# A fused attention and gated-MLP kernel: four engines in a hand-written order instead of one

## The chip, the cores and the metric

The kernel runs on one core of one Trainium2 chip. The metric is the device time of one execution in microseconds (us); lower is better. The profile gives a "span" (first to last instruction), which is about 2 us shorter than the time. The engines are named as in the profile: PE (TensorE, matrix multiplication), PEld (its weight loads), DVE (VectorE), ACT (ScalarE), POOL (GpSimd) and SP (SyncE, here used only to issue DMAs).

## The reference, cut to what matters

```python
# q, k, v: (B=8, H=8, S=576, D=64);  w_in: (512, 2048);  w_out: (2048, 512)
theta = pi/2 * arange(S) / S
phi(x) = concat([relu(x)*cos(theta), relu(x)*sin(theta)], axis=-1)   # 64 -> 128 features
kv  = einsum('bhsf,bhsd->bhfd', phi(k), v)          # per batch and head, 128 x 64
z   = sum over s of phi(k)
num = einsum('bhsf,bhfd->bhsd', phi(q), kv)
den = einsum('bhsf,bhf->bhs',  phi(q), z) + 1e-6
x   = (num / den), heads put side by side           # (4608 tokens, 512)
h   = x @ w_in
out = (h * cos(h)) @ w_out
```

Batches are independent of each other in the attention, so batch b+1's attention can be computed while batch b goes through the MLP. A batch has 576 tokens: four tiles of 128, and 64 left over, which two batches share as one "remainder" tile.

## The kernel before: the parts that the change touches

The work is organised in stages. Stage s runs the first layer (x @ w_in and the gate) of batch s, the second layer of batch s-1, and, placed between their matmuls, the attention of batch s+1. A first-layer tile is four matmuls of 512 columns, a second-layer tile is sixteen. The features and casts that the attention needs are these:

```python
def prep(b, name, dst, t):                 # features of k or q, one token tile
    in_ = raw[name][:, :, t, :]
    for g in range(2):                     # g=0: cos, g=1: sin
        sc = CS[:, b % 2, g, t:t + 1]
        if b == 0 and g == 1 and t % 5 in (0, 1, 3, 4):
            nc.scalar.activation(out=dst[:, t, :, g, :], in_=in_, func=AF.Relu, scale=sc)
        else:
            nc.vector.tensor_scalar(out=dst[:, t, :, g, :], in0=in_, ..., op0=ALU.max, op1=ALU.mult)

def prep_v(b):                             # v to f16; only batch 0 uses ScalarE
    for t in range(NT + 1):
        ...
        if b == 0 and t % 2 == 1: nc.scalar.activation(out=dst, in_=src, func=AF.Copy)
        else:                     nc.vector.tensor_copy(out=dst, in_=src)

def kv_group(b, hb):                       # needs the k features and v of all five token tiles
    ...
    for hh in range(HB):
        for t in range(NT + 1):
            nc.tensor.matmul(KV[:, hh, :], lhsT=kp[:, t, h]..., rhs=V1[b % 2][:, t, h, :], ...)

def gate(dst, M1, n):                      # h * cos(h), the cosine as a shifted sine
    nc.scalar.activation(out=ch[:, 0:n], in_=M1, func=AF.Sin, bias=PIH, scale=1.0)
    nc.vector.tensor_tensor(out=dst, in0=M1, in1=ch[:, 0:n], op=ALU.mult)
```

Only TensorE's order is written by hand; a scheduler orders the other engines. The attention's steps are spread over the MLP's steps by their number:

```python
for name in ("k", "q", "v"): ...           # first loads
...
with tc.manual_schedule(engines={mybir.EngineType.PE}):
    ...                                     # opening: batch 0's attention, first layer, batch 1's attention
    for s in range(1, B + 1):
        side = attention(s + 1) if s + 1 < B else []
        spread(mlp(s), (xr if s == 1 else []) + list(side))
```

## Time and profile before

| | before |
|---|---|
| time, median of 3 runs first taken | 328.23 us (327.62 to 328.58) |
| span of the profiled run | 325.8 us, mean granted TensorE clock 0.988 |
| busy | PE 291.2, DVE 204.8, ACT 145.2, POOL 7.9 us |
| stage 1 starts / stage 2 starts / last matmul ends | 69.95 / 97.73 / 321.0 us |

These are lines of the first parts of the profile's page for the kernel before: the span, the busy times, and three rows in which each digit is a fortieth of the span (8.1 us). The PE and ACT rows give the busy share in tenths, the PEclk row the clock that TensorE was granted, in tenths of full speed.

```profile
span 325.8 us, 5431 instructions
PE 291.2 (89%) x2100; PEld 153.1 (47%) x2100; DVE 204.8 (63%) x520; ACT 145.2 (45%) x225; POOL 7.9 (2%) x19
...
PE   0578799989679979999999999999989999999994
...
ACT  2844273566253524454454442554444444554111
...
PEclk9999899999799999999999999999999999999999
```

The PE row is 9 almost everywhere after the twelfth slice (one 7, at 114 to 122 us): from 98 us on, TensorE is the bound, and what can be gained there is small. The losses lie in front. The timeline of the kernel before shows them. Its columns are the start in us, the duration in us, the engine, the line of the kernel, the operation with its tiles and count, and in brackets how long the engine had idled before and what released it.

```profile
11.88 1.04 PE L135 MATMUL QP_0_124<-IDENT,qp_106 128*128 128x128 f16 x8 [11.88 <-ACT qp_106 L96]
...
37.25 0.88 DVE L98 TENSOR_SCALAR kp_334<-km,CS 128x512 f16<-128x512 f32 x2 [11.31 <-DMA km<-in_k_dram]
38.78 1.87 PE L237 MATMUL M_403<-xT_108,w_in_sb 128*128 128x512 f16 x4 [2.42 <-DVE g_338 L230]
...
85.71 0.30 PE L160 MATMUL NUM_0_0_978<-kvz_795,qT_849 128*128 128x65 f16 x4 [2.54 <-DMA qT_849<-qp_794]
97.73 1.02 PE L237 MATMUL M_1176<-xT_796,w_in_sb 128*128 128x512 f16 x4 [2.17 <-DMA xT_796<-x_3_1072]
```

DVE sat 11.31 us in batch 1's first k feature, whose data had not arrived, with batch 0's gates queued behind it; TensorE ran out of free output buffers (the program has eight) and waited 2.42 us. The tile after that wait took 1.87 us; a first-layer tile at full clock is listed with 1.02 to 1.04 us, or 0.865 us from start to start. In stage 1 TensorE waited 2.54 us for q transposed and, at the start of stage 2, 2.17 us for x transposed, both by DMA.

### The profile page before, as it was taken

The page shows a single profiled execution, that of the slowest core. Times are in us where ns is not written, and L with a number is a line of the kernel's source. Part 1 is how long each engine was busy: PE and PEld are TensorE (multiplying, and loading weights), DVE is VectorE, ACT ScalarE, POOL GpSimd, SP SyncE. Part 2 cuts the span into 40 slices and gives each one's busy share as a digit, 9 for nine tenths or more (in the row PEclk, how much of TensorE's full clock was granted, in tenths as well). Part 3 has the DMA queues.
Part 4 walks back from the last instruction along what each step waited for, and adds up shares of the span by engine and source line. Part 5 has one row for each costly group of instructions (what it writes and reads, how often), then busy time and mean ns, then how long its engine had stood idle before and what let it go on. Part 6 is the DMA issues. An engine that isn't in the chain of part 4 may idle for free.

```text
span 325.8 us, 5431 instructions
## 1 busy us (share of the span) xinstructions
PE 291.2 (89%) x2100; PEld 153.1 (47%) x2100; DVE 204.8 (63%) x520; ACT 145.2 (45%) x225; POOL 7.9 (2%) x19
## 2 busy tenths in 40 slices
PE   0578799989679979999999999999989999999994
PEld 0553245554354534445554544445734544446441
DVE  2941499599699699494977595578943752444000
ACT  2844273566253524454454442554444444554111
POOL 0800000000000000000000000000000000000000
PEclk9999899999799999999999999999999999999999
DMA  7999954929957968993599667963920241010221
GB/s 231 292 206 205 288 171 148 328 93 255 291 118 175 260 218 205 227 274 110 131 195 268 206 177 163 262 206 90 186 82 32 35 113 64 2 64 2 80 80 64
DMA packets 78680, 53.73 MB, mean 165 GB/s; under 512 B 47424, under 2 KB 76096, under 8 KB 78656
## 3 DMA queue, kind: packets, MB, share of 16 engines
q1 hardware_dynamic: 74144, 49.16, 54.6%
q0 software_dynamic: 4224, 4.19, 7.8%
q8 instruction: 16, 0.26, 0.3%
q10 hardware_dynamic: 288, 0.04, 0.1%
q14 instruction: 8, 0.07, 0.1%
HBM read 36.74 MB, written 9.44 MB: 142 GB/s over the span
## 4 chain that ended last, share of the span: by engine, by line
PE 66%; DVE 11%; DMA 9%; issue 6%; ACT 2%; POOL 1%; DVEq 0%; POOLq 0%
DMA qT_849<-qp_794 3%; DVE g_338 L230 3%; DMA qT_1216<-qp_1168 3%; DMA km<-in_k_dram 1%; ACT ch L229 1%; DVE kp_334 L98 1%; DVE qp_1581 L98 1%; PE M_723 L271 1%; PE M_2316 L271 1%; PE M_1458 L271 1%; DVE g_1175 L230 1%; PE M_3657 L271 1%; PE M_3618 L271 1%; PE M_3251 L271 1%; PE M_3168 L271 1%
## 5 line engine op out<-in xcount | busy, mean ns | idle before, releaser
L237 PEld LDWEIGHTS <-w_in_sb 128*128 128x128 f16 x512 | 49.1, 100 | 65.4 <-issue 14.0
L249 PEld LDWEIGHTS <-w_in_sb 128*128 128x128 f16 x256 | 14.6, 98 | 0.9
L98 DVE TENSOR_SCALAR kp_334<-km,CS 128x512 f16<-128x512 f32 x10 | 4.7, 476 | 11.3 <-DMA km<-in_k_dram 11.3
L135 PE MATMUL QP_0_124<-IDENT,qp_106 128*128 128x128 f16 x8 | 1.0, 311 | 11.9 <-ACT qp_106 L96 11.9
L271 PEld LDWEIGHTS <-g_806 128*128 128x128 f16 x64 | 6.3, 98 | 8.0 <-issue 0.7
L271 PEld LDWEIGHTS <-g_338 128*128 128x128 f16 x64 | 5.9, 98 | 8.4 <-DVE g_338 L230 1.3
L271 PEld LDWEIGHTS <-g_3290 128*128 128x128 f16 x64 | 6.3, 98 | 7.6
L135 PEld LDWEIGHTS <-qp_106 128*128 128x128 f16 x40 | 4.1, 147 | 12.2 <-ACT qp_106 L96 11.9
L271 PEld LDWEIGHTS <-g_1588 128*128 128x128 f16 x64 | 6.3, 98 | 7.5 <-issue 0.2
L271 PEld LDWEIGHTS <-g_1175 128*128 128x128 f16 x64 | 6.2, 98 | 7.3
L271 PEld LDWEIGHTS <-g_2033 128*128 128x128 f16 x64 | 6.2, 98 | 7.3
L271 PEld LDWEIGHTS <-g_2891 128*128 128x128 f16 x64 | 6.2, 98 | 7.3
L271 PEld LDWEIGHTS <-g_2446 128*128 128x128 f16 x64 | 6.2, 98 | 7.3
L108 DVE CAST V_1_72<-vm 128x512 f16<-128x512 f32 x20 | 7.2, 420 | 0.0
L98 DVE TENSOR_SCALAR kp_793<-km,CS 128x512 f16<-128x512 f32 x10 | 4.4, 480 | 3.9 <-PE KV_1_619 L116 3.9
L108 DVE CAST V_0_71<-vm 128x512 f16<-128x512 f32 x18 | 6.4, 420 | 0.0
L98 DVE TENSOR_SCALAR qp_1581<-qm,CS 128x512 f16<-128x512 f32 x10 | 4.2, 477 | 3.1 <-DMA qT_1216<-qp_1168 3.1
L98 DVE TENSOR_SCALAR kp_105<-km,CS 128x512 f16<-128x512 f32 x6 | 2.5, 482 | 5.4 <-DMA km<-in_k_dram 5.4
L98 DVE TENSOR_SCALAR qp_2884<-qm,CS 128x512 f16<-128x512 f32 x10 | 4.2, 476 | 1.9 <-DMA qT_2495<-qp_2439 1.9
L98 DVE TENSOR_SCALAR qp_1168<-qm,CS 128x512 f16<-128x512 f32 x10 | 4.4, 474 | 1.2 <-DMA qT_849<-qp_794 1.2
L230 DVE TENSOR_TENSOR g_3290<-M_3291,ch 128x512 f16<-128x512 f32 x1 | 0.7, 692 | 7.1 <-ACT ch L229 7.1
L98 DVE TENSOR_SCALAR qp_2439<-qm,CS 128x512 f16<-128x512 f32 x10 | 4.1, 479 | 1.5 <-DMA qT_2074<-qp_2026 1.5
(893 smaller groups left out, 721.1 us busy)
## 6 DMA issues: line engine op xcount, KB each, us to landing
out_dram<-ost SPq DMA_DIRECT2D x32, 256.0 KB, 2.4
km<-in_k_dram SPq DMA_DIRECT2D x8, 640.0 KB, 5.1
qm<-in_q_dram SPq DMA_DIRECT2D x8, 640.0 KB, 4.9
vm<-in_v_dram SPq DMA_DIRECT2D x8, 640.0 KB, 7.2
km<-in_k_dram SPq DMA_DIRECT2D x8, 512.0 KB, 5.4
qm<-in_q_dram SPq DMA_DIRECT2D x8, 512.0 KB, 5.4
vm<-in_v_dram SPq DMA_DIRECT2D x8, 512.0 KB, 8.6
w_in_sb<-in_moe_w_in_dram POOLq DMA_DIRECT2D x4, 512.0 KB, 8.8
```

The costliest lines, as they stand in the source:

```text
L98: nc.vector.tensor_scalar(out=dst[:, t, :, g, :], in0=in_, scalar1=0.0, scalar2=sc, op0=ALU.max, op1=ALU.mult)
L108: nc.vector.tensor_copy(out=dst, in_=src)
L135: nc.tensor.matmul(QP[:, h, :], lhsT=src[:, h].rearrange("p g d -> p (g d)"), rhs=IDENT, is_transpose=True)
L229: nc.scalar.activation(out=ch[:, 0:n], in_=M1, func=AF.Sin, bias=PIH, scale=1.0)
L230: nc.vector.tensor_tensor(out=dst, in0=M1, in1=ch[:, 0:n], op=ALU.mult)
L237: nc.tensor.matmul(M1, lhsT=w_in_sb[:, c, j * P:(j + 1) * P], rhs=xts[b][:, c, :], start=(c == 0), stop=(c == NCT - 1))
L249: nc.tensor.matmul(M1[:, jj, :], lhsT=w_in_sb[:, c, j * P:(j + 1) * P], rhs=xts[("r", pr)][:, c, :], start=(c == 0), stop=(c == NCT - 1))
L271: nc.tensor.matmul(M2, lhsT=gts[key][:, j, gsl], rhs=w_out_sb[:, j, :], start=(j == 0), stop=(j == NJT - 1))
```

## The change

The intent: close those holes. All four engines get a written order; the loads go k, v, q; batch 0's first layer begins on the first two token tiles; one second-layer tile (two in stage 1) is kept for each stage's end, to cover the transposes there; the attention's steps are placed by the TensorE time that has passed. To take load off DVE, half of the k features and all casts of v go to ScalarE in every stage. Stores move to GpSimd's queue, and the last tile's eviction is split between two engines. The core of the diff:

```diff
+    late = []                       # gate multiplies and num/den divisions are put off by one step
+    def flush(): ...
-    def prep(b, name, dst, t): ...
-    def prep_v(b): ...
+    def feat(b, name, t, g, act): ...          # act: on ScalarE, else on VectorE
+    def val(b, t, act): ...
...
-        nc.vector.tensor_tensor(out=dst, in0=M1, in1=ch[:, 0:n], op=ALU.mult)
+        flush()
+        late.append(lambda: nc.vector.tensor_tensor(out=dst, in0=M1, in1=ch[:, 0:n], op=ALU.mult))
...
-    def moe1(b, j):
+    def moe1(b, j, s0=0, s1=SM):               # first layer on a part of the tokens
...
+            eng = nc.sync if b == B - 1 else nc.gpsimd
...
     def spread(main, side):
-        (by number of steps)
+        side, at = list(side), 0.0
+        for us, f in main:
+            while side and side[0][0] <= at:
+                side.pop(0)[1]()
+            f()
+            at += us
...
-    for name in ("k", "q", "v"):
+    for name in ("k", "v", "q"):
...
-    with tc.manual_schedule(engines={mybir.EngineType.PE}):
+    with tc.manual_schedule(engines={ET.PE, ET.DVE, ET.Activation, ET.SP}):
+        ...                                     # opening, written out
+        for s in range(1, B + 1):
+            M1_US, M2_US, b = 0.87, 3.46, s + 1
+            m1 = [(M1_US, lambda j=j: moe1(s, j)) for j in range(NJT)] if s < B else []
+            ahead = 2 if s == 1 else 1
+            m2 = [(M2_US, lambda t=t: moe2_main(s - 1, t)) for t in range(2 if s == 2 else 1, NT)] if s > 1 else []
+            ...                                 # one m2 step after every `per` m1 steps
+            if s < B:
+                main += [(M2_US, lambda t=t: moe2_main(s, t)) for t in range(ahead)]
+            ...
+                for t in T1:
+                    side += [(1.1 * t, lambda t=t: feat(b, "q", t, 0, False)),
+                             (1.1 * t, lambda t=t: feat(b, "q", t, 1, False)),
+                             (6.5 + t, lambda t=t: feat(b, "k", t, 0, False)),
+                             (6.5 + t, lambda t=t: feat(b, "k", t, 1, True)),
+                             (7.0 + t, lambda t=t: val(b, t, True))]
+                side += [(5.5, lambda: q_trans_dma(b)), (5.6, lambda: load(b + 1, "q")),
+                         (11.6, lambda: load(b + 1, "k")), (11.6, lambda: load(b + 1, "v")),
+                         (13.0, lambda: kv_group(b, 0)), (14.0, lambda: kv_group(b, 1))]
+                side += [(16.5 + 1.3 * t, lambda t=t: num(b, t)) for t in range(NT + b % 2)]
+            side.sort(key=lambda x: x[0])
+            spread(main, side)
```

## The prediction

> **What bounds the kernel now.** The page gives a span of 325.8 us (median time 328.23), PE busy 291.2 (89%), DVE 204.8, ACT 145.2; the chain of waits is 66% PE. The PE timeline shows where PE is not busy: nothing before 11.88 us (first q transpose); cold matmuls until 31 us (a first-layer tile takes 1.6-1.9 us instead of 0.865); 2.42 us at 36 us, because DVE sat 11.3 us in a feature op waiting for batch 1's k while batch 0's gates queued behind it, and 1.7 us of slow clock after; in stage 1 (69.95-97.73) 2.54 us for qT, 2.17 us for xT, about 1.4 us of slow clock; 4.9 us after the last matmul. From 97.7 to 321.0 PE has only 5-6 us of holes.
>
> **What the change does.** TensorE work is nearly equal. Opening: k, v, q order lets KV start near 11.6 us; the first layer starts near 24 us on two token tiles (27.07 before); gates no longer sit behind batch 1's features, so batch 0's first layer should end near 40.5 us (47.2 before). Then ACT has five 1.0 us qT copies and two V casts ahead of KV, so about 2 us go again: stage 1 starts near 63.5 (69.95 before). Gain 6.5 us. Tail: split eviction and smaller stores, about 1 us. Waits for qT and xT are covered by a second-layer tile moved to each stage's end (worth 5-6 us), except at the end of stage 1, where x of three tiles is made inside one 3.46 us tile: 2-2.5 us stay.
>
> **What it costs.** Half of the k features and all V casts move from DVE to ACT, in a fixed order. On ACT one feature starts 0.62 us after the last, a V cast 0.52, a sine 0.60 (ACT timeline). In stages 2, 3 and 5 all ten stand behind the eviction of a second-layer tile. From that tile's end ACT needs 0.2+0.53+5x0.62+5x0.52+2 or 3 sines, 7.6-8.2 us, before the last V is cast; PE has only 4 or 5 first-layer tiles (3.5-4.3 us) before KV, which needs all five. Estimate: PE waits 4 us in stages 2, 3, 5, 2.5 us in 4 and 6, 3.5 us in stage 1: 17 us in stages 2-6 that the old order did not have. [...] here 2.42 us of idle was followed by tiles of 1.87 and 1.72 us. I add 0-7 us, 3 in the middle.
>
> **Sum (span).** 63.5 + stage 1 34.3 (now with two second-layer tiles) + stages 2-8 210 of work + 17 of waits + 3.7 tail = 328.5, plus 3 clock = 331; time = span + 2.4. Without the waits on ACT it would be about 313. Weighing that, I say 330 us, 8 in 10 between 316 and 341. Faster by over 2% 0.25, within 2% 0.43, slower 0.32.
>
> **What would show it.** PE timeline: in each of stages 1-6 an idle of 2.5-4 us at the first KV group, released by the ACT cast of V; tiles over 1.2 us right after. DVE busy down about 25 us, ACT up by the like. First layer starts at 22-25 us; no 11 us DVE wait for km; no PE wait on qT after stage 1; stores on the software DMA queue without effect.
>
> **What would make it wrong.** PE late at KV for other reasons, which hides the wait, or ACT casts cheaper: then 313-320. Clock dropping after every wait[...]: 340.

63.5 + 34.3 + 210 + 17 + 3.7 is 328.5 us, and with 3 us for the clock it was put at 331 us of span, or 333.4 us of time.

## The result, and the profile after

The changed kernel took 341.44 us (median of 4 runs, 339.96 to 343.24) against 328.40 us (327.62 to 328.65) for the kernel before on the same chip: the ratio is 1.040, with a 95% interval of 1.035 to 1.046, so it is slower. All eight runs are fast. Ratios in this document are the mean time of one kernel's fast runs over that of the other's in the same rounds, so they are not quite the ratio of the medians quoted. The predicted 330 us was too low, and 341.44 lies just outside the range of 316 to 341.

The same lines of the page, for the kernel after:

```profile
span 338.1 us, 5548 instructions
PE 294.8 (87%) x2124; PEld 157.9 (47%) x2124; DVE 188.1 (56%) x460; ACT 181.8 (54%) x298; POOL 29.2 (9%) x55
...
PE   0589997796979699968999799987999799999994
...
ACT  3598573689325832675426743567426843655211
...
PEclk9999997999979789996999899997999999999998
```

The opening is better: the first-layer work starts at 22.86 us instead of 27.07, and stage 1 at 62.97 us instead of 69.95. But the ACT row has become a comb: it rises to 7 or 8 and falls to 2 or 3 again once per stage. The PE and PEclk rows have gained dips at the same rhythm, where the kernel before had, from 98 us on, one dip in PE and none in PEclk. The table of waits of PE after (tile and line, what it waited for, sum in us, times, longest) gives the dips a name:

```profile
PE KV_0_2650 L121 <- ACT V_0_71 L112: 3.6, 3, 1.5
PE KV_0_1792 L121 <- ACT V_0_71 L112: 3.6, 3, 1.5
PE KV_0_1400 L121 <- ACT V_1_72 L112: 3.3, 3, 1.5
PE KV_0_1005 L121 <- ACT V_0_71 L112: 3.0, 2, 1.5
PE M_1262 L207 <- DMA xT_819<-x_3_1232: 2.5, 1, 2.5
PE KV_0_655 L121 <- ACT V_1_72 L112: 2.0, 2, 1.7
PE KV_0_2235 L121 <- ACT V_1_72 L112: 1.9, 2, 1.4
PE KV_0_3087 L121 <- ACT V_1_72 L112: 1.9, 2, 1.4
```

In stages 1 to 6 TensorE stops at the first matmuls of the KV group, until ScalarE has cast the next tile of v: 3.0 us in stage 1 and 14.3 us in stages 2 to 6. (KV_0_655, with 2.0 us, is batch 1's, in the opening.) Stage 3 shows how this comes about. The timeline of the kernel after, all engines, from the second-layer tile M_1721 to the slow tiles:

```profile
142.01 3.62 PE L233 MATMUL M_1721<-w_out_sb,g_1261 128*128 128x512 f16 x16
142.21 0.69 ACT L197 ACTIVATE ch<-M_1710,PIH 128x512 f32<-128x512 f32 x1 [0.17 <-PE M_1710 L207]
...
145.66 0.60 ACT L259 ACTIVATE ost<-M_1721 128x512 f32<-128x512 f32 x1 [2.77 <-PE M_1721 L233]
146.16 0.71 ACT L104 ACTIVATE kp_1647<-km,CS 128x512 f16<-128x512 f32 x1
...
146.77 0.62 ACT L112 ACTIVATE V_0_71<-vm 128x512 f16<-128x512 f32 x1
...
149.55 0.71 ACT L104 ACTIVATE kp_1647<-km,CS 128x512 f16<-128x512 f32 x1
149.70 0.19 PE L121 MATMUL KV_0_1792<-V_0_71,kp_1647 128*128 128x65 f16 x1 [0.56 <-ACT V_0_71 L112]
150.16 0.67 ACT L197 ACTIVATE ch<-M_1753,PIH 128x512 f32<-128x512 f32 x1
...
151.41 0.19 PE L121 MATMUL KV_0_1792<-V_0_71,kp_1647 128*128 128x65 f16 x1 [1.51 <-ACT V_0_71 L112]
...
152.44 0.62 ACT L112 ACTIVATE V_0_71<-vm 128x512 f16<-128x512 f32 x1
...
153.11 1.04 PE L121 MATMUL KV_0_1792<-V_0_71,kp_1647 128*128 128x65 f16 x16 [1.51 <-ACT V_0_71 L112]
...
153.96 1.90 PE L207 MATMUL M_1814<-xT_1258,w_in_sb 128*128 128x512 f16 x4
```

ScalarE sits idle for 2.77 us before it evicts M_1721 (the `ost` line at 145.66), although k and v have been there for long (the last load of them was issued at 117.16 us and took 9.9 us to land). It works through its queue in order here: in the 2.77 us nothing that stood behind the eviction was begun. Behind it stand five k features and five casts, mixed with the sines of the next tiles. They start one every 0.5 to 0.6 us, and the last cast begins at 152.44, 6.8 us after the eviction's start. TensorE meanwhile needs only four first-layer tiles, 145.46 to 148.91, before it reaches the KV group. The placement explains it: the list places a step when TensorE time has passed its mark, and it passes 6.5 to 9.5 us in one jump, over a tile of 3.46 us. So every k feature and cast marked in that interval is emitted after that tile's eviction. Four tiles later, at 13.0, the list emits KV.

The last line shows the second cost. M_1814 took 1.90 us instead of about 1.03, and the KV group before it 1.04 us instead of 0.64: TensorE runs at half speed after the wait, and the trace gives the granted clock as 0.50 from 151.63 to 158.46 us.

The budget of the span, read from where each stage's first tile starts in the two PE timelines. The work that the change moved into stage 1 (two second-layer tiles, 6.9 us, and the remainder's numerators, 0.5 us) is taken out of the comparison:

| part | before | after | after minus before |
|---|---|---|---|
| until stage 1 starts (less 0.5 moved out) | 69.95 | 62.97 | -6.5 |
| stage 1, 27.8 before, 34.2 - 7.4 after | 27.8 | 26.8 | -1.0 |
| stages 2 to 8, 223.3 - 6.9 before | 216.4 | 236.6 | +20.2 |
| after the last matmul | 4.8 | 4.35 | -0.5 |
| sum | | | +12.2 (spans: +12.3) |

The 20.2 us of stages 2 to 8 have two parts: 14.3 us of waits at KV, and 9.9 us that matmuls took longer than at full clock behind those waits and, 1.6 of the 9.9, behind the 2.46 us wait for x at the start of stage 2 (tiles of 1.2 to 1.9 us, KV groups of 1.04, and one second-layer tile of 4.98 instead of 3.62). Against these stand some 4 us of small waits that the kernel before had there and the new one has not.

### The profile page after: what moved, and what is told of

It reads as the page before. It is cut to its first block, busy times and chain, and to the rows that moved or that the text cites. A ratio compares the mean times of both kernels' runs of the same rounds, so it can differ in the third digit from the quotient of the medians.

```text
span 338.1 us, 5548 instructions
## 1 busy us (share of the span) xinstructions
PE 294.8 (87%) x2124; PEld 157.9 (47%) x2124; DVE 188.1 (56%) x460; ACT 181.8 (54%) x298; POOL 29.2 (9%) x55
## 4 chain that ended last, share of the span: by engine, by line
PE 64%; ACT 18%; DVE 10%; issue 3%; DMA 3%; SPq 0%; ACTq 0%; DVEq 0%
ACT ch L197 5%; ACT V_1_72 L112 2%; DMA vm<-in_v_dram 2%; ACT V_0_71 L112 2%; PE M_1430 L233 1%; ACT qT_514 L139 1%; PE M_699 L233 1%; DVE g_2512 L199 1%; DVE g_1654 L199 1%; ACT qT_108 L139 1%; PE M_3707 L233 1%; PE M_2995 L233 1%; PE M_2137 L233 1%; PE M_3645 L233 1%; PE M_3338 L233 1%
## 5 line engine op out<-in xcount | busy, mean ns | idle before, releaser
L207 PEld LDWEIGHTS <-w_in_sb 128*128 128x128 f16 x536 | 52.1, 100 | 60.8 <-issue 11.5
L265 POOL DMA_DIRECT2D out_dram<-ost x14 | 8.8, 629 | 235.6 <-ACT ost L259 235.6
L219 PEld LDWEIGHTS <-w_in_sb 128*128 128x128 f16 x256 | 14.5, 98 | 0.5
L121 PE MATMUL KV_0_125<-V_0_71,kp_105 128*128 128x65 f16 x20 | 1.6, 240 | 11.5 <-DVE V_0_71 L114 11.0
L112 ACT ACTIVATE V_1_72<-vm 128x512 f16<-128x512 f32 x17 | 10.7, 635 | 0.0
L112 ACT ACTIVATE V_0_71<-vm 128x512 f16<-128x512 f32 x17 | 10.5, 625 | 0.1
L233 PEld LDWEIGHTS <-g_822 128*128 128x128 f16 x64 | 6.5, 104 | 8.2 <-issue 2.4
L233 PEld LDWEIGHTS <-g_3357 128*128 128x128 f16 x64 | 6.3, 98 | 7.5
L233 PEld LDWEIGHTS <-g_2099 128*128 128x128 f16 x64 | 6.2, 98 | 7.3
L233 PEld LDWEIGHTS <-g_2957 128*128 128x128 f16 x64 | 6.2, 98 | 7.3
L233 PEld LDWEIGHTS <-g_1654 128*128 128x128 f16 x64 | 6.2, 98 | 7.3
L233 PEld LDWEIGHTS <-g_2512 128*128 128x128 f16 x64 | 6.2, 98 | 7.3
L233 PEld LDWEIGHTS <-g_322 128*128 128x128 f16 x64 | 6.2, 100 | 7.2 <-issue 0.6
L233 PEld LDWEIGHTS <-g_1261 128*128 128x128 f16 x64 | 6.2, 98 | 7.1
L266 POOL DMA_DIRECT2D out_dram<-ost x14 | 7.8, 557 | 0.0
L121 PEld LDWEIGHTS <-kp_105 128*128 128x128 f16 x40 | 2.3, 130 | 11.7 <-ACT kp_105 L104 11.0
L274 POOL DMA_DIRECT2D out_dram<-ostr x8 | 4.3, 546 | 36.2 <-ACT ostr L271 36.2
L104 ACT ACTIVATE kp_105<-km,CS 128x512 f16<-128x512 f32 x5 | 3.2, 708 | 4.5 <-DMA km<-in_k_dram 4.5
L233 PE MATMUL M_1430<-w_out_sb,g_822 128*128 128x512 f16 x16 | 5.0, 480 | 0.0
L121 PEld LDWEIGHTS <-kp_1647 128*128 128x128 f16 x40 | 2.7, 129 | 4.6 <-ACT kp_1647 L104 3.4
L121 PE MATMUL KV_0_1792<-V_0_71,kp_1647 128*128 128x65 f16 x20 | 1.6, 233 | 3.6 <-ACT V_0_71 L112 3.6
```

Of the source, the lines that this page charges most:

```text
L104: nc.scalar.activation(out=dst, in_=src, func=AF.Relu, scale=sc)
L121: nc.tensor.matmul(KV[:, hh, :], lhsT=kps[b][:, t, h].rearrange("p g d -> p (g d)"), rhs=V1[b % 2][:, t, h, :], start=(t == 0), stop=(t == ...
L207: nc.tensor.matmul(M1, lhsT=w_in_sb[:, c, j * P:(j + 1) * P], rhs=xts[b][:, c, s0:s1], start=(c == 0), stop=(c == NCT - 1))
L219: nc.tensor.matmul(M1[:, jj, :], lhsT=w_in_sb[:, c, j * P:(j + 1) * P], rhs=xts[("r", pr)][:, c, :], start=(c == 0), stop=(c == NCT - 1))
L233: nc.tensor.matmul(M2, lhsT=gts[key][:, j, gsl], rhs=w_out_sb[:, j, :], start=(j == 0), stop=(j == NJT - 1))
L265: eng.dma_start(out=five[:, t - 1:t + 1, :], in_=blocks(ost, n))
```

## The experiments

The theory (A): the placement puts ten ScalarE instructions behind one eviction, and TensorE pays twice, for the wait and for the clock after it. Rivals: (B) the DMA of v comes too late; (C) ScalarE has simply too much work, wherever it stands; (D) the lower clock is not a consequence of the waits. Edits are against the changed kernel. Medians are given with their range, and ratios are to the kernel before in the same rounds. Its medians were 328.15 us in the first call, 326.80 in the second and 327.31 in the third (7, 7 and 12 runs).

### e1_v_dve: the casts of v back on VectorE

```diff
-                             (7.0 + t, lambda t=t: val(b, t, True))]
+                             (7.0 + t, lambda t=t: val(b, t, False))]
```

> V casts of batches 2 to 7 back on VectorE, nothing else moved. Theory A (TensorE waits at the first KV group because ten ScalarE instructions stand in a fixed order behind a second-layer eviction): five instructions of 0.52 us are gone from that queue, so each KV wait falls by about 2.5 us: from 3.0-3.6 to about 1 us in stages 1, 2, 3, 5 and from 1.9 to 0 in 4 and 6; half-clock stretches mostly go; 322-329 us. Rival B (v itself lands late by DMA, behind the stores on the software queue or the q transposes): the waits stay and name the VectorE cast or the DMA of v; within 3 us of the changed kernel.

Measured: 324.75 us (324.16 to 325.39), ratio 0.989 (0.983 to 0.994). The waits at KV in stages 2 to 6 fell to one of 1.2 to 1.6 us each; in stages 4 and 6, where none was expected, 1.18 us stayed, released by a k feature on ScalarE. The timeline of this run, stage 3:

```profile
146.99 0.64 PE L121 MATMUL KV<-V,kp 128*128 128x65 f16 x16 [1.58 <-DVE V L114]
147.47 1.89 PE L207 MATMUL M<-xT,w_in_sb 128*128 128x512 f16 x8
```

This takes 30 casts, one per 0.52 us, or 15.6 us of work, off ScalarE and gains 16.7 us. The second line counts eight matmuls in 1.89 us, so they are at full speed: behind one wait of 1.58 us no matmul was slow. In stage 1 two waits of 0.80 and 1.14 us stayed, and a tile of 1.65 us followed. This speaks for A, but it also takes load off ScalarE, so C still stands.

### e2_early and e12_early_again: the same instructions on the same engines, placed earlier

```diff
-                             (6.5 + t, lambda t=t: feat(b, "k", t, 1, True)),
-                             (7.0 + t, lambda t=t: val(b, t, True))]
+                             (0.5 + 1.2 * t, lambda t=t: feat(b, "k", t, 1, True)),
+                             (1.0 + 1.2 * t, lambda t=t: val(b, t, True))]
```

> The same ten ScalarE instructions per stage on the same engine, placed from 0.5 us of TensorE time instead of from 6.5. Theory A (order, not load): waits at KV vanish in stages 2 to 6 and fall below 1.5 us in stage 1, the granted clock rises from 0.956 to about 0.98; 311-318 us. Rival C (ScalarE simply has too much to do in a stage): the sines come late instead and TensorE waits for PSUM buffers or second-layer inputs, 330 us or more. Rival B (v lands late): waits stay.

> The early placement again, for comparison within this call: 317-319 us.

Measured: 318.39 us (316.81 to 319.28), ratio 0.969 (0.962 to 0.976); repeated on another chip, 318.20 us (317.15 to 321.02), ratio 0.974 (0.971 to 0.978). The time is just above the 311 to 318 us expected, the waits are as expected but for stage 1 (see below). This is the decisive run. ScalarE is as busy as before the edit (179.2 us against 181.8), so C falls. The v loads are where they were, and from batch 2 on no KV wait on v was left, so B falls. The casts now stand between sines, one at a time. ScalarE's and TensorE's timeline of stage 3 in this run:

```profile
134.62 0.63 ACT L112 ACTIVATE V<-vm 128x512 f16<-128x512 f32 x1
135.13 0.69 ACT L197 ACTIVATE ch<-M,PIH 128x512 f32<-128x512 f32 x1
135.70 0.73 ACT L104 ACTIVATE kp<-km,CS 128x512 f16<-128x512 f32 x1
136.32 0.64 ACT L112 ACTIVATE V<-vm 128x512 f16<-128x512 f32 x1
```

```profile
139.58 3.62 PE L207 MATMUL M<-xT,w_in_sb 128*128 128x512 f16 x16
143.03 0.88 PE L121 MATMUL KV<-V,kp 128*128 128x65 f16 x20
143.75 1.89 PE L207 MATMUL M<-xT,w_in_sb 128*128 128x512 f16 x8
```

Twenty KV matmuls follow the four tiles without a bracket, and the two tiles after them take 1.89 us together. In stages 2 to 6 the waits at KV are at most 0.29 us. What is left is a wait of 0.22 + 1.40 us in stage 1 (released by a k feature on VectorE), 2.46 us for x at the start of stage 2, and 2.0 us at batch 1's KV in the opening, which the edit does not touch.

### e3_filler: the waits kept, but filled with dummy matmuls

Before each first KV group, 16 to 30 matmuls of 260 columns run into the KV tile, whose real result then starts afresh. They use only tiles that have long been ready. This gives the right result and moves no other engine.

```diff
+    FILL = {2: 26, 3: 30, 4: 30, 5: 16, 6: 30, 7: 16}
     def kv_group(b, hb):
         KV = ppool.tile(...)
+        if hb == 0:
+            for _ in range(FILL.get(b, 0)):
+                nc.tensor.matmul(KV.rearrange("p h d -> p (h d)"), lhsT=IDENT,
+                                 rhs=w_in_sb[:, 0, 0:HB * D1], start=True, stop=True)
```

> The changed kernel with 16 to 30 matmuls of no use (0.11 us each) ahead of the first KV group of batches 2 to 7, into the tile that the KV matmuls overwrite. ScalarE's queue and so the time at which V is there are untouched. Theory A with clock (an idle TensorE is given half clock, and that costs 8-10 us over the kernel): KV still ends at the same distance after its last V cast, tiles after it take 1.03 and not 1.9 us, 331-335 us, clock about 0.98. Rival D (the slow tiles come from something else than idling[...]): tiles stay slow, 340 us or more.

Measured: 332.87 us (331.00 to 333.61), ratio 1.012 (1.006 to 1.019). The timeline of PE in stage 3 of this run:

```profile
148.11 3.49 PE L122 MATMUL KV<-w_in_sb,IDENT 128*128 128x260 f16 x30
151.44 0.28 PE L128 MATMUL KV<-V,kp 128*128 128x65 f16 x4
152.31 0.64 PE L128 MATMUL KV<-V,kp 128*128 128x65 f16 x16 [0.59 <-ACT V L112]
152.79 1.89 PE L214 MATMUL M<-xT,w_in_sb 128*128 128x512 f16 x8
```

The KV group is done 8.1 us after the first tile behind the eviction, against 8.5 us before the edit: ScalarE is as late as ever. But the matmuls behind it run at full speed, and the kernel is 8.6 us faster (341.44 to 332.87) with more work. So the clock behind the KV waits costs about 9 us (8.6 by the medians, 9.2 by the two ratios to the kernel before, since these are different calls), close to the 8.3 us counted in the trace after (9.9 less the 1.6 behind the wait for x), and rival D, a lower clock for another reason, falls: keeping TensorE busy restores it.

### e4_pe_only: the scheduler orders all engines but TensorE again

```diff
-    with tc.manual_schedule(engines={ET.PE, ET.DVE, ET.Activation, ET.SP}):
+    with tc.manual_schedule(engines={ET.PE}):
```

> The changed program text with only TensorE's order fixed by hand, as before; VectorE, ScalarE and the DMA queue are ordered by the scheduler, which puts the k features and V casts of a batch on ScalarE up to a stage earlier. Theory A: waits at KV small, 310-322 us, unless an early cast that waits for its load blocks sines behind it. If the hand order were not the cause: about 341 us.

Measured: 335.78 us (334.61 to 336.02), ratio 1.021 (1.016 to 1.027), a miss. The KV waits of stages 1 to 6 are gone, as expected: TensorE's list alone does not cause them. This run frees VectorE, ScalarE and the DMA queue together; that it is ScalarE's order, e2_early shows. Two other holes came. TensorE's timeline of this run, and SP's:

```profile
39.09 6.12 PE L207 MATMUL M<-xT,w_in_sb 128*128 128x256 f16 x31 [12.34 <-DVE g L199]
...
113.80 7.37 PE L207 MATMUL M<-xT,w_in_sb 128*128 128x512 f16 x24 [11.29 <-DMA xT<-x]
```

```profile
98.28 4.14 SPq L169 DMA_TRANSPOSE xT<-x  x2
102.51 6.39 SPq L129 DMA_TRANSPOSE qT<-qp  x1
109.00 3.41 SPq L169 DMA_TRANSPOSE xT<-x  x2
```

The scheduler again put batch 1's k features ahead of batch 0's gates on DVE (it waited 13.73 us for the data), and on SP it put the transpose of the next q between the second and the third transpose of x, where 6.39 us passed before SP came to the x that TensorE was waiting for. So the written order is needed: with ScalarE's part of it mended (e2_early, 318.39) it is 17 us better than the scheduler's. Of the written order, ScalarE's part is what costs most; the 2.46 us wait for x at the start of stage 2 is a fault of the written order too and stays in e2_early.

### e5_stores_sp and e11_early_sp: the stores back on SP's queue

```diff
-            eng = nc.sync if b == B - 1 else nc.gpsimd
+            eng = nc.sync
...
-            nc.gpsimd.dma_start(out=five[:, NT, :], in_=blocks(ost, n))
+            nc.sync.dma_start(out=five[:, NT, :], in_=blocks(ost, n))
```

> The changed kernel with its output stores back on the SyncE queue, as before. If the stores on GpSimd's software queue do not matter (prediction and theory A): within 3 us of the changed kernel, 338-344 us, waits at KV unchanged. Rival: [...] 335 us or less.

> The early placement plus output stores on the SyncE queue: the test of the software queue again on the quieter base. If the queue does not matter: within 1 us of the early placement alone in this call. [...] If stores in SyncE's order delay loads and transposes behind them: 1-4 us slower.

Measured on the changed kernel: 339.04 us (335.78 to 342.56; one of four runs, 342.56, counted as slow; the three fast ones have a median of 337.90), ratio 1.034 (1.028 to 1.041). Measured with the edit of e2_early: 319.40 us (317.46 to 319.81), ratio 0.975 (0.973 to 0.978), beside 318.20 and 0.974 without it. The stores' queue makes no difference that these runs resolve. The KV waits were the same to 0.05 us. Of POOL's 29.2 us of busy time after (7.9 before), 20.9 us are the issues of these stores, and the tables of waits list no engine that waits for one of them.

The profiled run of e5_stores_sp showed something else. After the same waits of 0.27 + 1.51 + 1.52 us in stage 2, its KV group took 0.64 us and the tile behind it 1.03 us, where the kernel after had 1.03 and 1.90 us:

```profile
114.61 0.64 PE L121 MATMUL KV<-V,kp 128*128 128x65 f16 x16 [1.52 <-ACT V L112]
115.09 1.03 PE L207 MATMUL M<-xT,w_in_sb 128*128 128x512 f16 x4
```

In stage 5 both kernels had the slow group of 1.04 us. So the same waits are followed by slow matmuls in one run and not in another. That fits the scatter of 335.78 to 342.56 in this kernel.

### e6_full and e10_early_full: batch 0's first layer on all its tokens

```diff
-        for j in range(2):
-            moe1(0, j, 0, SM // 2)
         x_trans(0, 2)
-        ...                                # half tiles, then the other half
         x_trans(0, 3)
-        ...
-        for j in range(6, NJT):
+        for j in range(NJT):
             moe1(0, j)
```

> The changed kernel with batch 0's first layer started only when all four token tiles are transposed, each tile on 512 tokens. The start of the first layer should move from 22.9 to about 25.3 us and stage 1 with it: 342-344 us, 1.5 to 2.5 us more than the changed kernel. Rival (the half-token start gains nothing since batch 1's loads set the pace later): no difference within 1 us.

> The early placement plus the first layer of batch 0 on all four token tiles: the test of the half-token start again, on a base whose runs scatter less. First layer starts 2.0-2.5 us later than in the early placement alone; if that start is on the chain, the time is 1.5-2.5 us above it (same call), otherwise within 0.7 us.

Measured: 338.81 us (336.60 to 342.91; one of four runs, 342.91, counted as slow), ratio 1.036 (1.029 to 1.044), a miss and inconclusive, because this kernel's scatter is larger than the 1 to 3 us in question. So it was repeated with the edit of e2_early: 316.91 us (314.92 to 318.14), ratio 0.968 (0.965 to 0.971), against 318.20 and 0.974. The first layer starts later (25.50 against 23.59 us), and stage 1 too (63.21 against 62.09), yet the time is not longer, but 1.3 us less, which neither of the two expectations foresaw. The half-token start gains about 1 us at its place, and the runs do not show that any of it reaches the end.

### e7_kv_late: KV placed later, ScalarE untouched

```diff
-                         (13.0, lambda: kv_group(b, 0)), (14.0, lambda: kv_group(b, 1))]
+                         (13.0 if s == 1 else 17.0, lambda: kv_group(b, 0)),
+                         (14.0 if s == 1 else 17.5, lambda: kv_group(b, 1))]
...
-                side += [(16.5 + 1.3 * t, lambda t=t: num(b, t))
+                side += [(16.5 + 1.3 * t if s == 1 else 18.5 + t, lambda t=t: num(b, t))
```

> ScalarE's and VectorE's work for k and v stays where the change put it; TensorE's KV groups move from 13.0/14.0 to 17.0/17.5 us of TensorE time and the numerators to 18.5 and on, in stages 2 to 6. Theory A (TensorE comes too early for an in-order ScalarE): the wait can be filled with first- and second-layer tiles; waits at KV in stages 2 to 6 fall from 14 us in all to under 4, stage 1 keeps its 3 us; 317-327 us. Rival C (ScalarE has too much to do): the time is lost elsewhere, 335 us or more.

Measured: 324.07 us (323.55 to 324.55), ratio 0.992 (0.989 to 0.994), as expected. TensorE does other work while ScalarE catches up, and the KV waits of stages 2 to 6 are gone. A part comes back at the end of the stage, because the numerators are later too. TensorE's timeline of this run at the start of stage 3:

```profile
131.45 4.00 PE L207 MATMUL M<-xT,w_in_sb 128*128 128x512 f16 x9 [3.60 <-DMA xT<-x]
```

Nine matmuls in 4.00 us are at half speed. With e1, e2 and e7, three different ways to take the wait away, A stands: fewer casts on ScalarE, the same casts earlier, or their consumer later.

### e8_best and e9_best2: what else can be had

e8_best adds to e2_early: one more second-layer tile kept for each stage's end, KV of stage 1 later, batch 1's casts on VectorE and its x transposes earlier.

```diff
-            ahead = 2 if s == 1 else 1
+            ahead = 3 if s == 1 else 2
-                  for t in range(2 if s == 2 else 1, NT)] if s > 1 else []
+                  for t in range(3 if s == 2 else 2, NT)] if s > 1 else []
-            val(1, t, t > 2)
+            val(1, t, False)
-                         (13.0, lambda: kv_group(b, 0)), (14.0, lambda: kv_group(b, 1))]
+                         (15.4 if s == 1 else 13.0, lambda: kv_group(b, 0)),
+                         (16.2 if s == 1 else 14.0, lambda: kv_group(b, 1))]
...                                        # x_trans(1, 0..1) before the last quarter of a second-layer tile
```

> All the mended waits together: the early ScalarE placement, stage 1's KV at 15.4/16.2, one more second-layer tile kept for the end of each stage so that the x transposes land under it, batch 1's V casts all on VectorE, two of batch 1's x transposes ahead of the last quarter of a second-layer tile, the remainder's transpose 1.5 us later. Theory A: the early placement gave 318.4; less 2.5 us (xT wait at the start of stage 2), 1.6 us (KV in stage 1), 2 us and some slow clock (KV of batch 1), about 1 us (transposes): 308-313 us, no TensorE wait over 1.5 us after 25 us.

Measured: 318.18 us (316.98 to 319.32), ratio 0.974 (0.970 to 0.977), a miss: no better than e2_early. Stage 2 does start 3.8 us earlier (92.93 against 96.77), with one more second-layer tile (3.46 us) already done. In the two profiled runs, from first tile to first tile, stage 2 then takes 1.7 us longer than in e2_early, stage 3 2.7 us and stages 4 to 6 0.9 to 1.5 us each, and the gain is used up. The timeline of this run, end of stage 2:

```profile
118.07 5.96 SPq L169 DMA_TRANSPOSE xT<-x  x3
...
126.45 0.76 DVE L164 TENSOR_TENSOR x<-NUM,rec 128x256 f16<-128x256 f32 x2 [5.15 <-DMA xT<-x]
...
127.92 2.29 PE L207 MATMUL M<-xT,w_in_sb 128*128 128x512 f16 x5 [3.60 <-DMA xT<-x]
```

DVE waited 5.15 us for a buffer of x that a transpose still read, and TensorE 3.60 us for the same transposes. These four took 7.8 us from issue to landing, behind two loads of v; in stage 2 of the kernel after it was 2.4 us for three of four. Behind the wait ten first-layer tiles took 11.6 us instead of 8.6. On top of e8_best, e9_best2 gives x six buffers instead of four, loads v later, puts the numerators 0.3 to 0.7 us later and VectorE's k features 1 us earlier:

```diff
-(11.6, lambda: load(b + 1, "v")),
+(23.0, lambda: load(b + 1, "v")),
-x16 = apool.tile(..., tag="x16", bufs=4)
+x16 = apool.tile(..., tag="x16", bufs=6)
-(16.5 + 1.3 * t, lambda t=t: num(b, t))
+(16.5 + 1.3 * t if s == 1 else 17.2 + 1.2 * t, lambda t=t: num(b, t))
-(6.5 + t, lambda t=t: feat(b, "k", t, 0, False))
+(5.5 + t, lambda t=t: feat(b, "k", t, 0, False))
```

> The kernel with all the waits mended, and one more: in it the x transposes of a stage landed after 5.4 us instead of 2.4 behind the next loads of q, k and v, and stage 3 began with a wait of 3.6 us for xT and a stretch of half clock. Here the load of v comes after the numerators, x16 has six buffers, the numerators stand 0.7 us later and the VectorE half of the k features 1 us earlier. Theory (DMA burst in front of the x transposes): transposes at 2.5-3.5 us, the wait for xT at stage 3 under 1 us, 309-315 us. If the burst was not the cause: 317-320 us as before.

Measured: 316.87 us (316.10 to 319.22), ratio 0.971 (0.967 to 0.974), short of its expected 309 to 315. The waits for x are gone (the transposes land after 2.8 us instead of 5.4, both medians over all stages; which of the four edits did it was not tested), but TensorE now reaches KV earlier than ScalarE and VectorE are done, and waits 1.3 to 2.9 us there in stages 2, 3 and 5. The hole moves from one producer to the next. The three best kernels (e2_early, e9_best2, e10_early_full) all beat both original kernels, by about 3% the one before and by about 7% the one after, and the runs do not separate them clearly from each other.

## Why the prediction was wrong

| step of the prediction | predicted | measured | |
|---|---|---|---|
| first layer starts | 22 to 25 us | 22.86 us | right |
| batch 0's first layer ends | 40.5 us | 37.45 us | better than predicted |
| stage 1 starts | 63.5 us | 62.97 us | right |
| stage 1 lasts | 34.3 us | 34.2 us | right |
| waits at KV, stages 2 to 6 | 17 us | 14.3 us | right, a little high |
| wait at KV, stage 1 | 3.5 us | 3.0 us | right |
| wait for x at stage 2 | 2 to 2.5 us | 2.46 us | right |
| slow clock after waits | 0 to 7 us, 3 in the middle | 9.9 us counted in one trace, 8.6 us by e3_filler | **mis-sized** |
| tail after the last matmul | 3.7 us | 4.35 us | 0.65 short |
| DVE busy down, ACT up | 25 us, "the like" | 16.7 us down, 36.6 us up | direction right |
| stores without effect | yes | yes (e5, e11) | right |

The mechanism was predicted and is what the runs showed: the opening gains, ScalarE's queue takes it back at KV, and the sum is a loss. The step that failed is "I add 0-7 us, 3 in the middle". The term was mis-sized by a factor of about three. With 9.9 in its place the prediction's own sum gives a span of 338.4, where 338.1 was measured. That it fits so closely is partly luck: the waits at KV were put 2.7 us too high, and the work of stages 2 to 8 about 2.4 us too low (210 against 236.6 - 14.3 - 9.9 = 212.4).

Two arguments were missing from the term. First, the prediction had itself listed six places with a wait of 2 to 4 us in stages 2 to 6, and in the trace before two of three such waits (2.42 and 2.54 us, not 2.17) were followed by 1.4 to 1.7 us of slow clock each. Two thirds of six places at that price give an estimate of 6 us, and all six 9 us. The prediction's sentence "Clock dropping after every wait ... 340" named what came in four of the five stages 2 to 6, and treated it as the exception. Second, the prediction had no way to count a wait that comes in pieces. Here the wait was split by single KV matmuls into pieces of at most 1.52 us and TensorE still came out at half speed: a tile took 1.90 us after 0.56 + 1.51 + 1.51 us in stage 3. Pieces did not protect it there.

The weights were also off. The prediction's own sum is a time of 333.4 us (331 + 2.4), and it said 330. It gave 0.43 to "within 2%" and 0.32 to "slower", because it left room for a TensorE that arrives late at KV. The trace before shows TensorE at work nearly without holes from 98 us on, and nothing in the change delayed it.

One thing that no run was made for can be read from the traces. Stages 4 and 6 have the same waits (0.51 + 1.42 us). In stage 4 a tile of 1.90 us followed, in stage 6 a tile of 1.03, and so it was in stage 1 after 1.47 + 1.51 us. So the length of the wait alone did not decide it. The granted clock in the traces suggests what else may count. From stage 2 to the last matmul, the half-clock stretches of the kernel after begin at 97.02, 114.08, 151.63, 192.59 and 230.14 us, which are 5, 11, 12 and 11 steps of 3.413 us apart, and each lasts one or two such steps (3.413 or 6.827 us in the trace's record of the clock).

Cut into steps on this grid from 30 us to the last matmul, the traces of the kernels before and after have 162 steps at full clock. All 8 with 2.23 us or more in which no matmul ran were followed by a step at half clock, and none of the 154 with 2.16 us or less. (How long a matmul runs is estimated here from the spacing of dense matmuls in these traces: 0.216 us for 512 columns, 0.056 for 128 and 0.030 for 65 at full clock, twice that at half.) In the trace after, stage 4 had 2.27 us in one step, stage 6 at most 1.25 us, because the edge of a step cut its wait in two, stage 1 2.16 us and stage 2 2.25 us. In the trace before, the wait of 2.54 us left 2.73 us without a matmul in one step and that of 2.42 us 2.23 us, while that of 2.17 us, which fell across two steps, left at most 1.27 us and was followed by a tile of 1.02 us. This is a count over two traces: no run moved a wait against the grid on purpose.

What stays open: the profiled pair overstates the clock's part somewhat: it has clocks of 0.956 and 0.988, while over all runs the kernel before had 0.965 to 0.988 and the kernel after 0.947 to 0.957. And the gain of the half-token start could not be resolved below about 1 us.

## What to carry to other kernels

Place work for an in-order engine by what stands ahead of it in that engine's own queue, not by the time of another engine: a list that steps over a long tile at once puts everything due in that time behind the tile's eviction, while the engine idles. Ask of each consumer when the last of its producers can be done, counted from that eviction; here moving ten instructions forward, with the same load, turned a loss of 4% into a gain of 3% (e2_early). And count a wait of a matmul engine with what follows it: here each us of wait in stages 2 to 6 brought on average about 0.6 us of slow matmuls (8.6 over 14.3), in stage 6 none.
